# A scan with attention ahead of a mixture of experts: index casts paced, last routing cut finer, first slice halved, more identity products, fill split

## The chip, the cores and the metric

One core of a Trainium2 chip runs the program. The metric is the device time of one execution in microseconds (us); lower is better. The kernel before takes 640.82 us, the median of three runs (640.61 to 641.45).

## What is computed

Two stages follow each other. The first is a linear recurrence over 768 positions for 4 batches and 8 heads of 48 dimensions. Each position has a complex decay per dimension, normalised to a magnitude of at most 0.999; a 48x48 state per head is multiplied by it, the outer product of k and v is added, and the output is q times the state:

```
mag = sqrt(a_re**2 + a_im**2);  scale = minimum(mag, 0.999) / (mag + 1e-6)
for t: S = (a_re + i*a_im)*scale [t] * S + outer(k[t], v[t]);  y[t] = q[t] @ S.real
```

The outputs, seen as 3072 tokens of 384 values, go to the second stage. Each token picks the expert with the largest of 8 logits (x @ w_gate); an expert takes its tokens in order up to a capacity. A token's result is its gate weight times relu(x @ w1[e]) @ w2[e], with 1024 hidden values, and rows beyond the capacity give zero:

```
e = argmax(logits);  gate = softmax(logits)[e];  disp[e, counts[e]++] = x[i]
out[i] = gate[i] * (relu(disp @ w1[e]) @ w2[e])[row of i]
```

## The kernel before

The recurrence is done in chunks of 96 positions (8 chunks per batch). Inside a chunk it becomes an attention-like product, for which the running products of the decays from the chunk's middle are needed. They are made by a scan of 48 steps, for two chunks at a time: this is group g = 0 to 3, 128 partitions wide. A group is cut into six slices of eight steps. For each slice `norm` (lines 278 to 378) loads the decays (`a`), squares them (L305), sums real and imaginary squares (L310 on VectorE for the first slice of all, L272 by two products with the identity on TensorE for the others), takes logarithm and exponential on ScalarE (L329 to L348) and scales on VectorE (L344 to L364); L369 and L374 copy signs and real parts. `scan` (L404, L409) does the steps, one product and one sum each, every step after the one before. `post` multiplies q and k by the scanned products (L452 to L487) and writes them to a scratch in HBM (`scr<-qko`, issued by POOL). `pend` and `ends` hand the last products over.

The second part of a group is its eight units (`unit`, one batch of one chunk each): load q, k and v rows (`qkc<-scr`, issued by SP), transpose (L629), score (L645), mask (L649), the state (L660, L669, and the accumulating transfers `z<-sx`, L673, from POOL), outputs (L706, L711), gate logits (L924) and a transpose back into token rows (L911). The units of group g run beside the scan of group g + 1.

Tokens are routed in pieces, listed in `CUTS` as (group, units done): all eight units at once in groups 0 to 2, and 5, 1, 1 and 1 units in group 3. `routing` (L730) makes logits (L952), choice (L960 to L965), counts by products with ones (L970 to L975), slots (L983 to L986), gate weights (L996 to L1006) and then for each unit a one-column cast of the slot to an index (L1010, VectorE) and a scatter of its 96 rows into `disp` in HBM (L1024, an indirect transfer issued by POOL). The last three pieces (`LATE`) do not have to come back from HBM: the first expert's rows are read from `disp` once (`mload`, L1074, issued by SP after all scatters of the other pieces), and the rows of the late pieces are added by products (L1088) to the transposed ones (L1094). Before the scatters `disp` is filled with zeros by seven transfers (`fill`, L853, 772 KB each, from POOL).

Then the experts run one after the other with their weights split in two parts each (L1129, L1130): L1220 is the first product, L1266 and L1267 the relu, L1228 (L1241 for the last expert) the second product, and L1185 scatters finished rows to the output.

What sets the order is a planner. Every operation is entered with an engine, an estimated duration, a due time (`want`), what it comes after and the buffers that it uses. `solve` simulates the engines by these estimates and fixes the order of the instructions on every engine; at run time each engine works through its list and waits on semaphores. `apart` (L96) keeps an operation's planned start a given time behind that of another one; nothing of it remains at run time but the order. `BEGIN` holds the due times at which the groups' scans begin. `fill_gaps` (L158) puts products of the identity with itself (`keep`, L226) where TensorE's plan has a gap of more than 0.4 us, from planned time `begin` on. When operation 60 of the order has been written out, `tokens` and the routing's constants (lines 1508 to 1511) are written into every engine's list at that place. Up to there the memsets of `clear_ops` are written, one after every second operation, into POOL's list.

Of the kernel before, what the change touches and what calls it, by code (L numbers as in the profile page):

```python
# [7 lines left out]
F32 = mybir.dt.float32  # L8
# [17 lines left out]
SIZES = (8,) * 6  # L26
# [22 lines left out]
class Plan:  # L49
# [20 lines left out]
    def ready(self, o, by):  # L70
        r = o.start + o.dur
        if by.begun and o.kb is not None:
            return r
        if o.lat is not None:
            return r + o.lat
        return r + (self.OWN if o.eng == by.eng else self.LAT)[o.eng]
# [96 lines left out]
def dve(n):  # L173
    return .068 + n * .00104


def act(n):
    return .045 + n * .00086


class Att:
# [94 lines left out]
        return out  # L276

    def norm(self, g, j, s0):

        nc, plan = self.nc, self.plan  # L280
        n = SIZES[j]
# [22 lines left out]
                st[0] = sq[:, 0]  # L304
            nc.scalar.activation(sq, st['a'], AF.Square, accum_out=self.sums[g][:, 0, j:j + 1])  # L305
        o = plan.op(K + ("xa",), "ACT", act(2 * n * D) + .1, xa, w, after=[K + ("load",)], bufs=[a_, a4_])
        if g == 0 and j < 1:
            def xb():
                x = self.a4[g, j][:, 0:n, 3, :]
                nc.vector.tensor_tensor(out=x, in0=st['sq'][:, 0], in1=st['sq'][:, 1], op=ALU.add)  # L310
                st[0] = x
            o = plan.op(None, "DVE", dve(n * D), xb, w, after=[o], bufs=[a4_])
            parts = [(0, n, o, a4_)]
        elif by_dma:
            def acc():
                nc.gpsimd.dma_start(out=st['flat'][:, 0], in_=st['flat'][:, 1], accum_op=ALU.add)
            o = plan.op(K + ("acc",), "POOL", .6, acc, w - 2, after=[o], bufs=[a4_], kb=24 * n, extra=3.)
            parts = [(0, n, o, a4_)]
        else:
            parts = self.sums_of(plan, K, lambda: (st['sq'][:, 0], st['sq'][:, 1]), n, [o], w, st, [a4_])  # L320
# [60 lines left out]
    def scan(self, g, j, wants):  # L381

        nc, plan = self.nc, self.plan
        K = ("n", g, j)
        n = SIZES[j]
        a4_ = ("a4", g, j)
        for s in range(n - 1, -1, -1):
            if j == 0 and s == n - 1:
                continue
            st = {}  # L390
            prev = (g, j, s + 1) if s < n - 1 else (g, j - 1, 0)
            want = wants[STARTS[j] + s]

            def parts(o, f):
                for cs in ((slice(0, D),) if o.form == "full" else (slice(0, D // 2), slice(D // 2, D))):
                    f(cs)

            def mul(cs, s=s, st=st, prev=prev):
                a4 = self.a4[g, j]
                if 'xy' not in st:  # L400
                    st['xy'] = self.p_t.tile([128, 4, D], F32, tag="xy", name=f"xy_{g}_{j}_{s}", bufs=RINGS["xy"])
                w = self.a4[prev[0], prev[1]][:, prev[2], 0:2, cs]
                w = w.unsqueeze(1).broadcast_to([128, 2] + list(w.shape[1:]))
                nc.vector.tensor_tensor(out=st['xy'][:, :, cs].rearrange("p (u z) d -> p u z d", u=2),  # L404
                                        in0=a4[:, s, :, cs].rearrange("p (u z) d -> p u z d", u=2), in1=w, op=ALU.mult)

            def add(cs, s=s, st=st):
                xy = st['xy']
                nc.vector.tensor_tensor(out=self.a4[g, j][:, s, 0:2, cs], in0=xy[:, 0:4:2, cs], in1=xy[:, 1:4:2, cs], op=ALU.add)  # L409
            xy_ = ("xy", g, j, s)  # L410
            bufs = [a4_, xy_] + ([("a4", g, j - 1)] if s == n - 1 else [])
            before = [("s", g) + prev[1:]] if ("s", g) + prev[1:] in plan.names else []
            m = plan.op(None, "DVE", .27, None, want, after=before + [K + ("i",), K + ("r",)], bufs=bufs)
            a = plan.op(("s", g, j, s), "DVE", .169, None, want, after=[m], bufs=[a4_, xy_])
            m.fn, a.fn = lambda m=m, f=mul: parts(m, f), lambda a=a, f=add: parts(a, f)
            m.form = a.form = "?"
            m.full, m.part, a.full, a.part = .269, .338, .169, .24
            m.next, a.next = [a], []
            for x in before:
                plan.names[x].next.append(m)  # L420
# [309 lines left out]
    def routing(self, b, c, w, span):  # L730
        plan, rt = self.plan, self.route
        c0 = rt.begin(b, c)
        n = c + 1 - c0
        fs = rt.route(b, c0, c + 1)
        K = lambda s: ("r", b, c, s)
        W = n * E_
        gs, xs = ([("u", i % B, G2 * b + i // B, x) for i in range(c0, c + 1)] for x in ("G", "X"))
        s = span / 8
        t0, t1 = ("tr", "lg", b, c), ("tr", "pp", b, c)
        prev = [("r",) + PREV[b, c + 1] + ("run",)] if (b, c + 1) in PREV else []  # L740
        o = plan.op(None, "PE", .12 * n + .1, fs['logits'], w, after=gs, bufs=[t0])
        o = plan.op(None, "ACT", act(W) + .1, fs['lg'], w + s, after=[o], bufs=[t0])
        o = plan.op(None, "DVE", 4 * dve(W) + .1 + .5, fs['choose'], w + 2 * s, after=[o])
        o = plan.op(None, "PE", .2 * n + .3, fs['count'], w + 3 * s, after=[o] + prev, bufs=[t1])
        e = plan.op(None, "ACT", act(W) + .1, fs['exp'], w + 2 * s, after=[o])
        o = plan.op(K("slot"), "DVE", 4 * dve(W) + .4, fs['slot'], w + 4 * s, after=[o], bufs=[t1])
        plan.op(K("run"), "DVE", 2 * dve(W) + .2, fs['run'], w + 4.2 * s, after=[o])
        o = plan.op(K("place"), "DVE", 2 * dve(W) + 1.0, fs['place'], w + 4.5 * s, after=[o, e] + xs)
        for i in range(n):
            x = plan.op(None, "DVE", .12, fs['cast'][i], w + (5 + i) * s, after=[o])  # L750
            o_ = plan.op(K(("send", i)), "POOL", 1.0, fs['send'][i], w + (5 + i) * s, after=[x] + ([("mload",)] if (b, c + 1) in LATE else []), kb=148, extra=2.)
            if rt.scattered is not None:
                o_.apart = (rt.scattered, APART[b])
            rt.scattered = o_


RINGS = dict(qkc=3, v=3, qT=2, kT=2, a_sb=2, z=5, s_sb=4, sx=4, xt=2, tr=2, pa=2, s=1, ad=2, y=1,
# [1 line left out]
RINGS.update(raw=3, raw1=3, ends=1)  # L759
SLATE = 6  # L760
NACC = 4
BEGIN = (13, 67, 135, 203, 271)
FIRST = 8
BEHIND = 6
APART = (5, 5, 2.6, 1)


E_, F_ = 8, 1024
# [14 lines left out]
    return p, [min(p, w - t) for t in range(0, w, p)]  # L783


CUTS = [(0, 8), (1, 8), (2, 8), (3, 5), (3, 6), (3, 7), (3, 8)]
LATE = CUTS[-3:]
PREV = {b: (a[0], a[1] - 1) for a, b in zip(CUTS, CUTS[1:])}

# [247 lines left out]
class Moe:  # L1037
# [33 lines left out]
    def load(self):  # L1071

        nc = self.nc
        nc.sync.dma_start(out=self.xr, in_=self.disp[:T, :].rearrange("(t p) x -> p t x", p=TP))  # L1074
# [391 lines left out]
def kernel(ctx, tc, q, k, v, a_re, a_im, w_gate, w1, w2, av, xv, cen, vp, out):  # L1466
# [5 lines left out]
    with ExitStack() as c_main, ExitStack() as c_att:  # L1472
# [18 lines left out]
        box = {'route': route}  # L1491
        moe_plan(plan, box, early)
        for r in range(E_ * T // 512):
            plan.op(("fill", r), "POOL", .9, lambda r=r: box['fill'][r](), 9 + 3 * r, kb=772)
        order = plan.solve()
        plan.fill_gaps(att.keep)
        cut = max(i for i, o in enumerate(order) if o.idx < early) + 1
        with ExitStack() as c_moe:
            with ExitStack() as c_dve:
# [116 lines left out]
```

## Time and profile before

| | us |
|---|---|
| median of 3 runs | 640.82 |
| the profiled execution | 641.58 |
| its span, first to last instruction | 639.9 |

| engine | busy us | share of the span |
|---|---|---|
| TensorE (PE) | 561.8 | 88% |
| VectorE (DVE) | 458.9 | 72% |
| ScalarE (ACT) | 383.5 | 60% |
| GpSimd (POOL) | 212.9 | 33% |

The mean granted TensorE clock is 0.936 of 2.4 GHz. All times below are from the first instruction of the profiled execution on. A row of the timeline gives start, duration, engine, line, operation, output and inputs, the number of instructions merged into it, and in brackets how long its engine stood idle before it and what ended that. PEld is the load of TensorE's stationary operand, SPq and POOLq are the queues that issue transfers. "issue" is time in which an engine waited for nothing that the profile shows; "remote" marks a wait whose releaser is not seen on another engine.

### The profile page before, as it was taken

To read this page: it belongs to the slowest core of one execution; us is meant where nothing else is said; L and a number is where in the kernel's file an instruction comes from. 1 tells how busy PE (TensorE), PEld (TensorE's weight loads), DVE (VectorE), ACT (ScalarE), POOL (GpSimd) and SP (SyncE) were. 2 spreads that over 40 slices of the span, in tenths; PEclk is the share of its full clock that TensorE was granted. 3 is DMA by queue.
4 is the path that set the end of the run, shared out by engine and by line. 5 is a ranking of instruction groups with operands and counts; after the bars stand their busy time and mean duration, and the time that the engine had idled before them with its cause. 6 is when DMAs were issued, how large, how long until landed. Compare 5 with 4: busy or idle time off the path is not lost.

```text
span 639.9 us, 13273 instructions
## 1 busy us (share of the span) xinstructions
PE 561.8 (88%) x4662; PEld 489.7 (77%) x4662; DVE 458.9 (72%) x1340; ACT 383.5 (60%) x1034; POOL 212.9 (33%) x293
## 2 busy tenths in 40 slices
PE   2364569998999989999896889999999999999994
PEld 1122258786887868888785877999999999999993
DVE  3899979999999998999763244546665655655651
ACT  6465689989998899977652421344445344444540
POOL 9532314524459925464525031002020202112012
PEclk9666679999999999999999779999999999999997
DMA  6985588968899787885997231364545454455311
GB/s 214 297 245 147 147 203 231 241 189 207 196 230 251 213 228 168 213 223 135 215 242 209 55 91 29 109 184 125 163 129 158 138 169 155 155 165 159 101 37 37
DMA packets 75629, 108.81 MB, mean 170 GB/s; under 512 B 11716, under 2 KB 65853, under 8 KB 75553
## 3 DMA queue, kind: packets, MB, share of 16 engines
q1 hardware_dynamic: 58192, 57.37, 33.3%
q0 software_dynamic: 17360, 50.50, 29.1%
q8 instruction: 39, 0.64, 0.4%
q14 instruction: 38, 0.30, 0.2%
HBM read 71.51 MB, written 32.47 MB: 163 GB/s over the span
## 4 chain that ended last, share of the span: by engine, by line
PE 55%; DVE 20%; DMA 10%; ACT 9%; issue 4%; POOL 1%; POOLq 0%; DVEq 0%; ACTq 0%; SPq 0%
PE ph L1220 17%; PE my L1228 15%; DVE xy L404 4%; DMA scr<-qko 3%; DVE a L409 3%; PE pa L645 3%; PE tr L629 2%; DMA raw<-in_moe_w_dram 2%; PE n L272 2%; PE my L1241 2%; DMA qkc<-scr 2%; DVE qko L452 2%; PE s_all L660 2%; PE y L706 2%; DMA a<-in_av_dram 2%
## 5 line engine op out<-in xcount | busy, mean ns | idle before, releaser
L1266 ACT ACTIVATE hh<-ph 128x448 fp32r<-128x448 f32 (+7 forms) x64 | 32.7, 511 | 92.1 <-PE ph L1220 81.8
L1267 DVE SCALAR_TENSOR_TENSOR hl<-ph,hh 128x448 fp32r<-128x448 f32 (+7 forms) x64 | 37.2, 581 | 60.4 <-ACT hh L1266 59.6
L1185 POOL DMA_INDIRECT out_dram<-o,xr x26 | 25.7, 987 | 162.8 <-DVE o L1184 159.5
L1130 DVE TENSOR_TENSOR lo<-raw,hi 128x384 fp32r<-128x384 f32 (+2 forms) x128 | 65.7, 553 | 9.8 <-ACT hi L1129 9.7
L272 PE MATMUL n<-a,ident 128*128 128x384 f32 x92 | 44.8, 622 | 28.7 <-ACT a L305 28.7
L1220 PE MATMUL ph<-xh,hi 128*128 128x448 f32 (+7 forms) x192 | 69.5, 362 | 0.0
L1220 PE MATMUL ph<-xh,lo 128*128 128x448 f32 (+7 forms) x192 | 66.5, 347 | 0.0
L404 DVE TENSOR_TENSOR xy<-a 128x192 f32<-128x192 f32 (+1 forms) x199 | 61.5, 322 | 1.3 <-ACT a L374 1.1
L1129 ACT CAST hi<-raw 128x384 fp32r<-128x384 f32 (+2 forms) x128 | 59.1, 512 | 2.8 <-DMA raw<-in_moe_w_dram 2.8
L673 POOL DMA_DIRECT2D z<-sx x56 | 47.4, 1003 | 39.8 <-PE pa L645 12.4
L629 PE MATMUL tr<-ident,qkc 81*96 81x81 f32 x512 | 53.8, 241 | 5.6 <-DMA qkc<-scr 2.6
L1228 PE MATMUL my<-hh,lo 128*128 128x448 f32 (+6 forms) x168 | 58.7, 349 | 0.0
L1228 PE MATMUL my<-hh,hi 128*128 128x448 f32 (+6 forms) x168 | 58.6, 349 | 0.0
L1228 PE MATMUL my<-hl,hi 128*128 128x448 f32 (+6 forms) x168 | 58.6, 349 | 0.0
L649 DVE TENSOR_TENSOR a_sb<-pa,mask 96x384 f32<-96x384 f32 x64 | 35.1, 552 | 32.1 <-PE pa L645 21.1
L1024 POOL DMA_INDIRECT disp<-x,idx x32 | 42.1, 1315 | 46.1 <-DVE lm L961 22.4
L645 PE MATMUL pa<-qT,kT 128*96 128x96 f32 x512 | 56.9, 256 | 0.5 <-issue 0.4
L629 PEld LDWEIGHTS tr<-ident,qkc 81*96 81x96 f32 x512 | 43.3, 130 | 13.3 <-issue 4.0
L645 PEld LDWEIGHTS pa<-qT,kT 128*96 128x96 f32 x512 | 51.2, 170 | 2.5 <-issue 1.6
L272 PEld LDWEIGHTS n<-a,ident 128*128 128x128 f32 x92 | 20.0, 237 | 42.8 <-ACT a L305 24.6
L272 PE MATMUL p<-qko,ident 128*128 128x384 f32 x80 | 37.4, 598 | 15.3 <-ACT qko L441 15.2
L409 DVE TENSOR_TENSOR a<-xy 128x96 f32<-128x96 f32 (+1 forms) x218 | 49.8, 240 | 0.4
(224 smaller groups left out, 1459.0 us busy)
## 6 DMA issues: line engine op xcount, KB each, us to landing
raw<-in_moe_w_dram SPq DMA_DIRECT2D x64, 384.0 KB
qkc<-scr SPq DMA_DIRECT2D x32, 480.0 KB
scr<-qko POOLq DMA_DIRECT2D x44, 192.0 KB
scr<-qko POOLq DMA_DIRECT2D x20, 384.0 KB
a<-in_av_dram POOLq DMA_DIRECT2D x18, 384.0 KB
qkin<-in_xv_dram POOLq DMA_DIRECT2D x18, 384.0 KB
disp<-fill POOLq DMA_DIRECT2D x7, 772.0 KB
v<-in_vp_dram SPq DMA_DIRECT2D x32, 144.0 KB
```

The source lines that it names most:

```text
L272: nc.tensor.matmul(out=pt[:, :m], lhsT=self.ident, rhs=t[:, h:h + m], start=i == 0, stop=i == 1)
L404: nc.vector.tensor_tensor(out=st['xy'][:, :, cs].rearrange("p (u z) d -> p u z d", u=2), in0=a4[:, s, :, cs].rearrange("p (u z) d -> p u z ...
L409: nc.vector.tensor_tensor(out=self.a4[g, j][:, s, 0:2, cs], in0=xy[:, 0:4:2, cs], in1=xy[:, 1:4:2, cs], op=ALU.add)
L629: nc.tensor.transpose(out=pt[:, h * C:h * C + NE], in_=qk[:NE, 4 * hh + h, z_ * C:z_ * C + C], identity=self.ident[:NE, :NE])
L645: nc.tensor.matmul(out=pa[:, h * C:h * C + C], lhsT=kT[:, 4 * hh + h], rhs=qT[:, 4 * hh + h], start=True, stop=True)
L673: nc.gpsimd.dma_start(out=zn[a.start:a.stop or C], in_=st['sx'][o], accum_op=ALU.add)
L1024: ins = nc.gpsimd.indirect_dma_start(out=self.disp, out_offset=bass.IndirectOffsetOnAxis(ap=idx[:, c:c + 1], axis=0), in_=self.row(b, c0 + ...
L1129: return (lambda: nc.scalar.copy(out=hi[i][:, s], in_=raw[i][:, s]), lambda: nc.vector.tensor_tensor(out=lo[i][:, s], in0=raw[i][:, s], in ...
L1130: lambda: nc.vector.tensor_tensor(out=lo[i][:, s], in0=raw[i][:, s], in1=hi[i][:, s].bitcast(F32), op=ALU.subtract))
L1220: nc.tensor.matmul(out=ph[:, :W], lhsT=a[:, k, fs], rhs=r[:, k, :W], start=i == 0, stop=i == len(parts) - 1)
L1228: nc.tensor.matmul(out=py[m][:, :W], lhsT=a[:, f % self.PF, ms], rhs=r[:, :W], start=f == 0 and i == 0, stop=f == NF - 1 and i == 2)
L1267: nc.vector.scalar_tensor_tensor(out=hl[:, :W], in0=ph[:, :W], scalar=0.0, in1=hh[:, :W].bitcast(F32), op0=ALU.max, op1=ALU.subtract)
```

## The change

- The distance `apart` is taken between the casts of the indices on VectorE, no longer between the scatters on POOL, and its values for groups 2 and 3 go from 2.6 and 1 to 2 and 1.4 us.
- The first routing of group 3 takes four units, and the fifth gets a piece of its own (`CUTS`).
- The first slice of group 0 has a function of its own, `norm_first`: it loads and normalises the eight steps in two halves of four, upper half first; every operation of `norm` for that slice is done twice on half the columns, and a scan step waits for its own half only.
- The groups' due times begin 3 us earlier (`BEGIN`).
- Identity products fill planned gaps from planned time 58 on, not 82.
- The seven fills have due times of their own (`FILL`).

```diff
     def norm(self, g, j, s0):
+        if g == 0 and j == 0:
+            self.norm_first(s0)
+        else:
+            self.norm_slice(g, j, s0)
+
+    def norm_first(self, s0):
...
+        n = SIZES[0]
+        w = s0 - 10
...
+        for p, h in enumerate(range(n - HALF, -1, -HALF)):
+            i = slice(h, h + HALF)
+            m = HALF * D
+            v = w + 4 * p
+
+            def load(i=i, p=p):
+                if p == 0:
+                    tiles_()
+                nc.sync.dma_start(out=st['a'][:, :, i], in_=self.av[0][:, :, STARTS[0] + i.start:STARTS[0] + i.stop, :])
+
+            def xa(i=i, p=p):
+                sq = st['a4'][:, i, 0:2, :].rearrange("p i z d -> p z i d")
+                nc.scalar.activation(sq, st['a'][:, :, i], AF.Square, accum_out=sums[:, 0, NS + p:NS + p + 1])
...
+            o = plan.op(K + ("load", p), "SP", .6, load, v - 14, bufs=[a_], kb=48 * HALF, extra=2.)
+            o = plan.op(K + ("xa", p), "ACT", act(2 * m) + .1, xa, v, after=[o], bufs=[a_, a4_])
+            x_ = plan.op(None, "DVE", dve(m), xb, v, after=[o], bufs=[a4_])
+            o = plan.op(None, "ACT", act(m), xc, v, after=[x_], bufs=[a4_, ln_, c0_, t5_])
+            e = plan.op(None, "ACT", act(m), xe, v, after=[o], bufs=[ln_, c0_])
+            o = plan.op(None, "ACT", act(m) + .1, xq, v, after=[e], bufs=[ln_, c0_])
+            o = plan.op(None, "DVE", dve(m), mm, v + 4, after=[o], bufs=[a4_, ln_])
+            t = plan.op(None, "ACT", act(m), tt, v + 4, after=[e], bufs=[c0_, t5_])
+            o = plan.op(None, "DVE", dve(m), c1, v + 5, after=[o, t], bufs=[ln_, c0_])
+            o = plan.op(None, "DVE", dve(m), sc, v + 6, after=[o, t], bufs=[c0_, t5_])
+            oi = plan.op(None, "DVE", dve(m), mi, v + 7, after=[o], bufs=[a_, t5_, a4_])
+            orr = plan.op(None, "DVE", dve(m), mr, v + 7, after=[o], bufs=[a_, t5_, a4_])
+            plan.op(K + ("i", p), "ACT", act(m) + .08 * (p == 0), ci, v + 7.5, after=[oi], bufs=[a4_])
+            plan.op(K + ("r", p), "ACT", act(m), cr, v + 7.5, after=[orr], bufs=[a4_])
...
+        def ready(s):
+            p = ((n - 1 - s) // HALF,) if g == 0 and j == 0 else ()
+            return [K + ("i",) + p, K + ("r",) + p]
...
-            m = plan.op(None, "DVE", .27, None, want, after=before + [K + ("i",), K + ("r",)], bufs=bufs)
+            m = plan.op(None, "DVE", .27, None, want, after=before + ready(s), bufs=bufs)
...
             x = plan.op(None, "DVE", .12, fs['cast'][i], w + (5 + i) * s, after=[o])
-            o_ = plan.op(K(("send", i)), "POOL", 1.0, fs['send'][i], w + (5 + i) * s, after=[x] + ([("mload",)] if (b, c + 1) in LATE else []), kb=148, extra=2.)
+            plan.op(K(("send", i)), "POOL", 1.0, fs['send'][i], w + (5 + i) * s, after=[x] + ([("mload",)] if (b, c + 1) in LATE else []), kb=148, extra=2.)
             if rt.scattered is not None:
-                o_.apart = (rt.scattered, APART[b])
-            rt.scattered = o_
+                x.apart = (rt.scattered, APART[b])
+            rt.scattered = x
...
-BEGIN = (13, 67, 135, 203, 271)
+FILL = (9, 13, 17, 21, 43, 47, 62)
+HALF = 4
+BEGIN = (10, 64, 132, 200, 268)
...
-APART = (5, 5, 2.6, 1)
+APART = (5, 5, 2, 1.4)
...
-CUTS = [(0, 8), (1, 8), (2, 8), (3, 5), (3, 6), (3, 7), (3, 8)]
+CUTS = [(0, 8), (1, 8), (2, 8), (3, 4), (3, 5), (3, 6), (3, 7), (3, 8)]
...
-            plan.op(("fill", r), "POOL", .9, lambda r=r: box['fill'][r](), 9 + 3 * r, kb=772)
+            plan.op(("fill", r), "POOL", .9, lambda r=r: box['fill'][r](), FILL[r], kb=772)
         order = plan.solve()
-        plan.fill_gaps(att.keep)
+        plan.fill_gaps(att.keep, begin=58.)
```

## Rows read from the trace of the kernel before

**Rows 1.** Windows: stretch and its length, then busy us (instructions) by engine, clock, DMA.

```profile
23.00:72.00 49.00, 23.15 (x37) 10.75 (x38) 48.64 (x174) 30.08 (x63) 14.81 (x28) 0.67 0.70 205
72.00:92.00 20.00, 13.10 (x49) 8.24 (x49) 16.38 (x54) 14.16 (x35) 6.29 (x9) 0.63 0.89 221
92.00:345.00 253.00, 241.95 (x2837) 205.35 (x2836) 232.20 (x702) 211.44 (x644) 129.67 (x154) 0.99 0.84 209
345.00:352.00 7.00, 1.34 (x10) 0.93 (x10) 0.00 (x0) 0.42 (x1) 5.33 (x6) 0.84 0.69 221
352.00:360.00 8.00, 6.39 (x60) 5.82 (x60) 1.11 (x2) 2.78 (x9) 0.00 (x0) 0.50 0.36 89
360.00:374.00 14.00, 13.88 (x192) 12.32 (x189) 7.42 (x43) 6.66 (x21) 2.77 (x3) 1.00 0.11 33
...
399.00:632.00 233.00, 231.69 (x1316) 225.20 (x1314) 133.95 (x285) 99.65 (x221) 28.52 (x30) 1.00 0.45 135
```

**Rows 2.** Timeline from 342 to 353 us: first and last of eight scatters, then what follows.

```profile
342.19 1.04 POOL L1024 DMA_INDIRECT disp<-x,idx  x1 [0.30 <-DVE a_sb L649]
...
350.93 0.92 POOL L1024 DMA_INDIRECT disp<-x,idx  x1 [0.30 <-issue]
351.58 0.48 ACT L900 COPY xt<-y 128x384 f32<-128x384 f32 x1 [8.34 <-remote]
...
352.12 0.55 PE L924 MATMUL y<-xt,wg 128*32 128x96 f32 x8 [5.37 <-issue]
```

**Rows 3.** Timeline from 375 to 390 us: last of five scatters, read-back, its first use.

```profile
375.38 0.92 POOL L1024 DMA_INDIRECT disp<-x,idx  x1 [0.30 <-ACT qT L633]
...
377.99 0.32 SPq L1074 DMA_DIRECT2D xr<-disp  x1
...
389.50 1.12 PE L1094 MATMUL mt<-ident,xr 112*128 112x112 f32 x8
```

**Rows 4.** Timeline of L924, once per unit, after the row of 352.12.

```profile
361.58 0.37 PE L924 MATMUL y<-xt,wg 128*32 128x96 f32 x8
...
367.10 0.37 PE L924 MATMUL y<-xt,wg 128*32 128x96 f32 x8
...
379.18 0.55 PE L924 MATMUL y<-xt,wg 128*32 128x96 f32 x8
...
385.75 0.37 PE L924 MATMUL y<-xt,wg 128*32 128x96 f32 x8
```

**Rows 5.** Timeline: first and last of four scatters among the experts; the window around them.

```profile
584.87 0.95 POOL L1185 DMA_INDIRECT out_dram<-o,xr  x1 [21.70 <-DVE o L1184]
...
589.90 0.94 POOL L1185 DMA_INDIRECT out_dram<-o,xr  x1 [0.30 <-issue]
...
584.00:591.00 7.00, 7.00 (x45) 6.92 (x43) 4.21 (x9) 1.80 (x4) 3.79 (x4) 1.00 0.77 231
```

**Rows 6.** Timeline of the start, then groups by line: count, busy us and mean ns.

```profile
4.72 0.84 ACT L305 ACTIVATE a<-a 128x768 f32<-128x768 f32 x1 [2.61 <-DMA a<-in_av_dram]
...
13.04 0.43 DVE L404 TENSOR_TENSOR xy<-a 128x96 f32<-128x96 f32 x2 [1.12 <-ACT a L374]
...
21.10 0.23 POOL L837 IOTA tok<- 96x32 int32 x1
...
22.38 0.25 DVE L242 TENSOR_TENSOR mask<-ptok,tokrow 96x96 f32<-96x96 f32 x1 [2.33 <-ACT tokcol L241]
...
L853 POOL DMA_DIRECT2D disp<-fill x7 | 5.7, 863 | 0.0
L487 DVE TENSOR_TENSOR qko<-a,v 128x768 f32<-128x768 f32 x6 | 5.7, 957 | 0.0
L344 DVE TENSOR_TENSOR lnn<-n,lnn 128x384 f32<-128x384 f32 x7 | 3.9, 553 | 0.0
```

**Rows 7.** Chain of waits: the sums' products at the handover, and later.

```profile
74.45 2.93 PE n L272 x4
...
127.64 1.35 PE n L272 x4
```

More of the change, by code (lines that the diff above doesn't have):

```diff
@@ L278, in norm, with tiles_, xb, xc @@
     def norm(self, g, j, s0):
+        if g == 0 and j == 0:
[3 more added lines that the diff above has]
+    def norm_first(self, s0):
+        nc, plan = self.nc, self.plan
+        n = SIZES[0]
+        w = s0 - 10
+        K = ("n", 0, 0)
+        sums = self.sums[0]
+        st = {}
+        def tiles_():
+            st['a4'] = self.tile_a4(0, 0)
+            st['a'] = self.p_in.tile([128, 2, n, D], F32, tag="a", name="a_0_0", bufs=RINGS["a"])
+            for x in ("ln", "c0", "t5"):
+                st[x] = self.p_t.tile([128, n, D], F32, tag=x, name=f"{x}n_0_0", bufs=RINGS[x])
+        a_, a4_, ln_, c0_, t5_ = ("a", K), ("a4", 0, 0), ("ln", K), ("c0", K), ("t5", K)
+        for p, h in enumerate(range(n - HALF, -1, -HALF)):
[9 more added lines that the diff above has]
+                nc.scalar.activation(sq, st['a'][:, :, i], AF.Square, accum_out=sums[:, 0, NS + p:NS + p + 1])
+            def xb(i=i):
+                nc.vector.tensor_tensor(out=st['a4'][:, i, 3, :], in0=st['a4'][:, i, 0, :], in1=st['a4'][:, i, 1, :], op=ALU.add)
+            def xc(i=i):
+                nc.scalar.activation(st['ln'][:, i], st['a4'][:, i, 3, :], AF.Ln, bias=self.b_tiny)
+            def xe(i=i):
+                nc.scalar.activation(st['c0'][:, i], st['ln'][:, i], AF.Exp, bias=self.b_lncap, scale=-0.5)
+            def xq(i=i):
+                nc.scalar.activation(st['ln'][:, i], st['c0'][:, i], AF.Square, scale=1.0 / CAP,
+                                     accum_out=sums[:, 1, self.col[0]:self.col[0] + 1])
+                self.col[0] += 1
+            def mm(i=i):
+                nc.vector.tensor_tensor(out=st['ln'][:, i], in0=st['a4'][:, i, 3, :], in1=st['ln'][:, i], op=ALU.mult)
+            def tt(i=i):
+                nc.scalar.activation(st['t5'][:, i], st['c0'][:, i], AF.Identity, bias=self.b_half, scale=0.5e-6 / CAP)
+            def c1(i=i):
+                nc.vector.scalar_tensor_tensor(out=st['c0'][:, i], in0=st['ln'][:, i], scalar=-3.0, in1=st['c0'][:, i], op0=ALU.add, op1=ALU.mult)
+            def sc(i=i):
+                nc.vector.scalar_tensor_tensor(out=st['t5'][:, i], in0=st['c0'][:, i], scalar=-2.0, in1=st['t5'][:, i], op0=ALU.max, op1=ALU.mult)
+            def mi(i=i):
+                nc.vector.scalar_tensor_tensor(out=st['a4'][:, i, 2, :], in0=st['a'][:, 1, i], scalar=self.sign[:, 0:1], in1=st['t5'][:, i],
+                                               op0=ALU.mult, op1=ALU.mult)
+            def mr(i=i):
+                nc.vector.tensor_tensor(out=st['a4'][:, i, 0, :], in0=st['a'][:, 0, i], in1=st['t5'][:, i], op=ALU.mult)
+            def ci(i=i, p=p):
+                k = i.stop - (p == 0)
+                nc.scalar.mul(out=st['a4'][:, i.start:k, 1, :], in_=st['a4'][:, i.start:k, 2, :], mul=-1.0)
+                if p == 0:
+                    nc.scalar.copy(out=st['a4'][:, k, 1, :], in_=st['a4'][:, k, 2, :])
+            def cr(i=i):
+                nc.scalar.copy(out=st['a4'][:, i, 3, :], in_=st['a4'][:, i, 0, :])
+            o = plan.op(K + ("load", p), "SP", .6, load, v - 14, bufs=[a_], kb=48 * HALF, extra=2.)
[12 more added lines that the diff above has]
+            plan.op(K + ("r", p), "ACT", act(m), cr, v + 7.5, after=[orr], bufs=[a4_])
@@ L280, in norm, with norm_slice @@
+    def norm_slice(self, g, j, s0):
         nc, plan = self.nc, self.plan
@@ L306, in norm @@
         o = plan.op(K + ("xa",), "ACT", act(2 * n * D) + .1, xa, w, after=[K + ("load",)], bufs=[a_, a4_])
[L307 to L314, printed above, removed]
+        if by_dma:
             def acc():
```

## The prediction

> **What bounds the kernel now.** I read the windows by stage first. In the experts TensorE is busy 231.69 of 233 us and the change touches nothing there, so that stage is a constant. Before it there are four stages [rows 1]. From 23 to 72 us VectorE is the bound: 48.64 of 49 us busy, TensorE less than half. From 72 to 92 us nobody is full: that is the handover from the first scan to the first units, at a granted clock of 0.63. From 92 to 345 us TensorE is busy 241.95 of 253 us and VectorE 232.20, so a start that comes earlier is passed on here, neither lost nor enlarged. From 345 to 399 us comes the surprise: in the seven microseconds to 352 VectorE does nothing, ScalarE 0.42 and TensorE 1.34 us, and the eight after it run at clock 0.50, while 360 to 374 shows TensorE busy 13.88 of 14 at 1.00.
>
> The timeline tells what goes on beside that hole. POOL issues eight scatters in one train, from 342.19 to 351.85, (350.93 - 342.19) / 7 = 1.25 us apart, since all eight indices were cast together; ScalarE's next copy starts at 351.58 after 8.34 us of idleness with no releaser on another engine, TensorE's next work at 352.12 after 5.37 us of "issue" [rows 2]. What stops the engines is not named by any view; I go by the coincidence, which comes twice: a train of five scatters ends at 376.30, and the unit it falls into is long again [rows 3, 4]. L924 runs once per unit and serves as a clock: 352.12, 361.58, 367.10, 379.18, 385.75, so the units last 9.46, 5.52, 12.08 and 6.57 us [rows 2, 4].
>
> **The change, part by part.** All sums are on the profiled execution, 641.58 us; its span is 639.9.
>
> *Casts paced, routing in pieces of four and one.* No cast is added; each moves down VectorE's list, to planned distances of 2 us (group 2) and 1.4 us (group 3), and POOL's scatter waits for its own. Does a train with such distances still stop the others? The trace has no such train in this stage. The nearest row is among the experts: four scatters start between 584.87 and 589.90, 1.68 us apart on the mean, and TensorE is busy 7.00 of 7.00 us around them [rows 5]. So at 2 us I expect no hole, and at 1.4 us a smaller one.
>
> What the holes cost: take 5.52 us as a unit without disturbance; it even contains a five-unit routing. The first hole is 7.00 - 1.34 = 5.66 us of TensorE, and the slow unit behind it 9.46 - 5.52 = 3.94; together 9.6. The second costs 12.08 - 5.52 = 6.56 and 6.57 - 5.52 = 1.05; together 7.6. All of it is 17.2 us, the upper end; the lower is 0. I take the first whole (8 scatters spread over 14 us) and half of the second, 3.8, because four scatters may still come in a row at 1.4 us: 13.4 us gained.
>
> The piece more is one more round of choice, counts, slots and weights on VectorE (idle half of 360 to 374, 7.42 of 14 [rows 1]) and two pairs of small products. 6.57 - 5.52 = 1.05 us is the most that a unit with a one-unit routing shows [rows 4]; between 0 and that I take 0.4 us lost.
>
> What the pacing could make late: the scatter waits for its cast, and behind it on POOL wait the state's transfers and the scratch writes; on SP `mload` waits for the last scatter of the early pieces. In groups 0 and 1 the planned 5 us were the scatters' own before; VectorE is nearly full there, so a cast that slips holds POOL, which is busy 129.67 of 253 us [rows 1]: 0, at most about 2 us. In group 3 the read-back is issued at 377.99 and first used at 389.50, 11.5 us later [rows 3]. With TensorE 13.4 us earlier that cover would be gone, but the fifth unit's piece now needs one scatter instead of five, and the four start one unit, 5.5 us, earlier; I count 0 and keep up to 3 us for the range.
>
> *First slice in two halves.* From the first square at 4.72 to the first scan step at 13.04 there are 8.3 us of operations one behind the other [rows 6]. On VectorE 768 columns take 0.957 and 384 take 0.553 us, so 192 take some 0.553 - 0.202 = 0.35, 0.63 of the whole. The chain shrinks to 5.3 us, and half a load may land 0.5 us sooner: the scan starts 3.5 us earlier. The second halves cost VectorE six times 2 x 0.35 - 0.553 = 0.15, 0.9 us, in time that it idles. But the constants stand in every list at operation 60, and the 14 operations more push that place forward. VectorE reached it at 20.05 and waited 2.33 us [rows 6]. Half of 14 operations at some 0.35 us is 2.5; with the 3.5 of the start it arrives at about 14. POOL finishes the last constant at 21.10 + 0.23; with three fills of 0.86 us fewer ahead of it, at 18.7 [rows 6]. So the wait grows to nearly 5 us. It ends 3.5 to 4 us earlier than before, with two scan steps and three scaling operations (2.4 us) still to do. Net 1.5 us gained; between -1 (POOL not earlier) and 3.5 (no wait).
>
> *Fills.* Seven as before, 0.86 us each on POOL; three move from 15-27 us to 43-62, where VectorE is the bound and POOL is busy 14.81 of 49 us [rows 1]. Beyond the constants' wait they are worth nothing: 0, with up to 0.5 either way inside the range above.
>
> *Identity products from 58 on.* They go into TensorE's idle time ahead of 72 us and through the handover. There the sums' products take 2.93 us on the chain and 1.35 at the higher of the two clocks (1.2 and 2.4 GHz) [rows 7]; two such sets (74.45 and 85.62) lie on the chain, 3.2 us. Upper end: half of TensorE's 13.10 us, 6.5. Lower end: -1, if the products themselves run at the low clock and hold up a sum behind them. ScalarE (14.16 of 20) and the read-back of the first units, with DMA at 0.89, are next [rows 1], so I take 2.0.
>
> In 72 to 92 us TensorE also does transposes. The Trainium skill, page "TensorE: Matmul & The Clock Gate", section "Part 4: PE-mode transpose", says that transposes do not count as activity for the clock. From 352 to 360 us TensorE was busy 6.39 of 8 us, transposes among it, and stayed at 0.50 [rows 1], which fits but does not separate it. By that rule the second set falls back to the low clock and the term is half, 1.0.
>
> *Sum.* 13.4 - 0.4 + 1.5 + 2.0 = 16.5; 641.58 - 16.5 = 625.1. The profiled execution is 0.76 above the median, so I say 624.3 for the median.
>
> **The rivals.** *The second train still stops the engines* (four at 1.4 us are close to the 1.25 of before; for it: the distance hardly grew; against: rows 5): 3.8 less, 628.1.
>
> *The casts bunch.* The pace exists only in the plan; if VectorE waits for TensorE with several casts behind the wait, they come together and POOL sends a train as before. For it: from 360 to 374 VectorE idles half its time [rows 1]. Against: each wait lets through only what stands between two masks. Then only start and clock remain: 641.58 - 3.5 + 0.4 - 0.76 = 637.7.
>
> *The transposes keep the handover slow* (above): 625.3.
>
> *Slower: every scatter stops the others while POOL writes it, whatever the distance.* In place of two holes there would be 13 of 0.92 us, 12.0 us, and TensorE interrupted every 2 us would stay at the low clock, 3.94 us for each unit. It beats the 17.2 us of now, and the 3.5 of start and clock, from (17.2 + 3.5 - 12.0) / 3.94 = 2.2 units on; over four units it is 12.0 + 15.8 = 27.8: 641.58 + 27.8 - 17.2 - 3.5 + 0.4 - 0.76 = 648.3. Against: the four scatters of rows 5 leave TensorE full.
>
> *The change does not do what it says*: the plan puts the casts apart and VectorE's order shows it, so I give that nothing beyond the bunching.
>
> **How the numbers follow.** My forecast 56%, the transposes' rival 10%, the second train 17%, bunching 10%, slower 7%. Low end: 17.2 + 3.5 + 3.2 = 23.9 gained, 616.9. High end: the bunching's 637.7, cut to 637; what is left out is the slower case and the worse half of bunching with a poor start. The likeliest case's own range is 619 to 631. About 0.2%, 1.3 us, is what a measurement here tells from no change. Faster by more: 56 + 10 + 17 and most of bunching, 0.89. Within 0.2%: bunching with the start lost, 0.04. Slower: 0.07.
>
> **What would show it.** Right: scatters of group 2 start 2 us apart, ScalarE shows no "remote" waits of several us, L924 comes every 5 to 6 us, the clock stays at 1.00 from 340 on; the first scan step is at 9 to 10 us, the wait at the mask near 5 us; sums near 1.4 us at the handover. Wrong: scatters 1.2 us apart, or holes despite the distance; the read-back's first use waiting for its landing; a stage 92 to 345 that grows by what its start gained.

## The result and the profile after

The changed kernel takes 623.96 us (median of 4 runs, 623.83 to 624.21) against 640.98 us (640.61 to 641.45) on the same chip: ratio 0.9735, 95% interval 0.9718 to 0.9751. Its profiled execution takes 624.08 us, with a span of 622.3 and a mean granted clock of 0.962. The forecast was 624.3.

In the profile after, the functions of the units and the routing stand 90 lines further down (L924 is L1014, L900 is L990, the scatter is L1114), masks are at L737 and scan steps at L492. Here are the windows that answer to [rows 1]; the experts now begin 17.9 us earlier.

```profile
72.00:92.00 20.00, 18.50 (x151) 15.36 (x150) 19.25 (x56) 17.18 (x45) 5.58 (x8) 0.96 0.85 226
345.00:352.00 7.00, 6.77 (x92) 6.08 (x88) 3.65 (x24) 3.29 (x12) 2.74 (x3) 1.00 0.42 119
352.00:360.00 8.00, 5.29 (x78) 4.76 (x78) 3.40 (x22) 2.82 (x10) 3.68 (x4) 1.00 0.20 59
360.00:374.00 14.00, 13.10 (x165) 11.51 (x164) 7.98 (x50) 4.54 (x15) 3.66 (x4) 1.00 0.34 97
```

Two things jump out. From 72 to 92 us TensorE went from 13.10 to 18.50 of 20 us and from clock 0.63 to 0.96; 7.0 of the 18.50 are identity products, of which the kernel before has none there. This group of instructions is from the window 72 to 92 us (count, busy us, mean ns):

```profile
L226 PE MATMUL s_all<-ident 128*128 128x128 f32 x47 | 7.0, 303 | 0.0
```

And the great hole is gone: TensorE has 6.77 of 7 us in the window to 352, at 1.00. A smaller one is left from 352 to 360, with 5.29 of 8. The timeline shows what lies in it (answer to [rows 2]): three scatters that do come together (the last of group 2's eight and the first two of group 3), and ScalarE and VectorE idle until 0.8 us after the last has ended.

```profile
353.08 0.92 POOL L1114 DMA_INDIRECT disp<-x,idx  x1 [2.05 <-DVE sl L1073]
354.49 0.93 POOL L1114 DMA_INDIRECT disp<-x,idx  x1 [0.49 <-DVE se L1088]
355.75 0.92 POOL L1114 DMA_INDIRECT disp<-x,idx  x1 [0.33 <-issue]
357.51 0.48 ACT L990 COPY xt<-y 128x384 f32<-128x384 f32 x1 [4.79 <-remote]
357.67 0.55 DVE L737 TENSOR_TENSOR a_sb<-pa,mask 96x384 f32<-96x384 f32 x1 [2.71 <-remote]
358.05 0.37 PE L1014 MATMUL y<-xt,wg 128*32 128x96 f32 x8 [2.33 <-ACT xt L990]
```

The scatters of group 2 are not evenly 2 us apart: their eight starts lie between 336.94 and 353.08, 1.27 to 3.85 us from one to the next. The first three stand 1.56 and 1.27 us apart, a first triplet.

At the start (answer to [rows 6]) the first square is at 3.87 and the first scan step at 10.25; the constants cost VectorE two waits of under 1 us.

```profile
3.87 0.52 ACT L311 ACTIVATE a<-a 128x384 f32<-128x384 f32 x1 [1.76 <-DMA a<-in_av_dram]
10.25 0.36 DVE L492 TENSOR_TENSOR xy<-a 128x192 f32<-128x192 f32 x1 [0.23 <-ACT a L353]
17.29 0.25 DVE L242 TENSOR_TENSOR mask<-ptok,tokrow 96x96 f32<-96x96 f32 x1 [0.79 <-ACT tokcol L241]
18.44 0.26 DVE L920 CAST dec<-ii 96x8 f32<-96x8 int32 x1 [0.90 <-POOL ii L917]
```

Three marks divide the gain: the third unit's first product (114.41 before, 109.08 after), the first product of the unit into which the train falls (L924 at 338.65, L1014 at 333.89), and the experts' first product (399.14 and 381.22). Here they are in the timeline, three before and three after:

```profile
114.41 0.37 PE L924 MATMUL y<-xt,wg 128*32 128x96 f32 x8
338.65 0.37 PE L924 MATMUL y<-xt,wg 128*32 128x96 f32 x8
399.14 0.45 PE L1220 MATMUL ph<-xh,hi 128*128 128x448 f32 x1
109.08 0.37 PE L1014 MATMUL y<-xt,wg 128*32 128x96 f32 x8
333.89 0.37 PE L1014 MATMUL y<-xt,wg 128*32 128x96 f32 x8
381.22 0.45 PE L1310 MATMUL ph<-xh,hi 128*128 128x448 f32 x1
```

So 5.3 us come from before 114 us, of which 4.8 are still there at 338.65; the scatter stage between the last two marks shrinks from 60.49 to 47.33 us, 13.2; the experts take 240.8 and 241.1 us. 4.76 + 13.16 - 0.32 = 17.60, the difference of the spans.

### The profile page after: what moved, and what is told of

It is laid out like the page before. It is cut to its first block, busy times and chain, and to the rows that moved or that the text cites. A ratio compares the mean times of both kernels' runs of the same rounds, so it can differ in the third digit from the quotient of the medians.

```text
span 622.3 us, 13489 instructions
## 1 busy us (share of the span) xinstructions
PE 558.7 (90%) x4740; PEld 491.0 (79%) x4740; DVE 462.7 (74%) x1366; ACT 383.6 (62%) x1045; POOL 209.5 (34%) x293
## 4 chain that ended last, share of the span: by engine, by line
PE 54%; DVE 19%; ACT 14%; DMA 5%; POOL 3%; issue 2%; another core or an unknown queue 1%; POOLq 0%; ACTq 0%; SPq 0%; DVEq 0%
PE ph L1310 17%; PE my L1318 15%; DVE xy L492 4%; DVE a L497 3%; ACT z L768 3%; PE pa L733 2%; DMA scr<-qko 2%; PE my L1331 2%; PE tr L717 2%; DVE qko L540 2%; ACT ends L615 2%; PE s_all L748 2%; PE y L794 1%; PE yt L1264 1%; DVE qko L575 1%
## 5 line engine op out<-in xcount | busy, mean ns | idle before, releaser
L492 DVE TENSOR_TENSOR xy<-a 128x192 f32<-128x192 f32 (+1 forms) x202 | 61.3, 318 | 0.8 <-ACT a L353 0.2
L272 PE MATMUL n<-a,ident 128*128 128x384 f32 x92 | 41.6, 585 | 16.9 <-POOL qT L246 8.9
L733 PE MATMUL pa<-qT,kT 128*96 128x96 f32 x512 | 55.0, 251 | 0.7 <-ACT kT L721 0.7
L717 PE MATMUL tr<-ident,qkc 81*96 81x81 f32 x512 | 52.5, 237 | 3.0 <-ACT x L1007 1.3
L1114 POOL DMA_INDIRECT disp<-x,idx x32 | 40.3, 1260 | 39.8 <-ACT lt L1017 9.5
L733 PEld LDWEIGHTS pa<-qT,kT 128*96 128x96 f32 x512 | 49.5, 166 | 2.9 <-ACT kT L721 1.1
L717 PEld LDWEIGHTS tr<-ident,qkc 81*96 81x96 f32 x512 | 41.6, 127 | 9.7 <-ACT x L1007 2.4
L737 DVE TENSOR_TENSOR a_sb<-pa,mask 96x384 f32<-96x384 f32 x64 | 35.1, 549 | 15.3 <-PE pa L733 10.9
L1310 PE MATMUL ph<-xl,hi 128*128 128x448 f32 (+7 forms) x192 | 45.8, 346 | 0.0
```

What stands on the lines that cost most here:

```text
L272: nc.tensor.matmul(out=pt[:, :m], lhsT=self.ident, rhs=t[:, h:h + m], start=i == 0, stop=i == 1)
L717: nc.tensor.transpose(out=pt[:, h * C:h * C + NE], in_=qk[:NE, 4 * hh + h, z_ * C:z_ * C + C], identity=self.ident[:NE, :NE])
L733: nc.tensor.matmul(out=pa[:, h * C:h * C + C], lhsT=kT[:, 4 * hh + h], rhs=qT[:, 4 * hh + h], start=True, stop=True)
L1114: ins = nc.gpsimd.indirect_dma_start(out=self.disp, out_offset=bass.IndirectOffsetOnAxis(ap=idx[:, c:c + 1], axis=0), in_=self.row(b, c0 + ...
L1310: nc.tensor.matmul(out=ph[:, :W], lhsT=a[:, k, fs], rhs=r[:, k, :W], start=i == 0, stop=i == len(parts) - 1)
```

## The experiments

Theory A is the prediction's: a train of scatters 1.25 us apart stops the other engines by itself. Its main rival, formed after the runs on chip 10 and called theory C from r2_before on, is that the stop is a condition of the chip or of the execution which a train meets or does not. (Rivals B and C in the expectations of e1 to e4 are others: that the finer pieces, or the start and the handover, bring the gain.) The runs went to chips 10, 5, 1 and 3 in that order, each chip once, and each has its own times of the kernel before; only ratios on one chip compare. The times expected for e1 to e4 were meant for the chip of the result, so on chip 10 their mechanisms can be tested, but not their microseconds.

**e1, trains again.** Casts together, distances on the scatters, as before the change; all else of the change stays.

```diff
-            plan.op(K(("send", i)), "POOL", 1.0, ...
+            o_ = plan.op(K(("send", i)), "POOL", 1.0, ...
             if rt.scattered is not None:
-                x.apart = (rt.scattered, APART[b])
-            rt.scattered = x
+                o_.apart = (rt.scattered, APART[b])
+            rt.scattered = o_
...
-APART = (5, 5, 2, 1.4)
+APART = (5, 5, 2.6, 1)
```

> The changed kernel with the distance back on the scatters (and its values 2.6 and 1), so that all indices of a piece are cast together; all else stays. Theory A (a train of scatters stops the other engines, and the distance between the casts is what takes the trains apart): the holes come back behind the eight scatters of group 2 and, smaller, behind the four of group 3; 633 to 637 us, with ScalarE waits marked remote of 5 us and more. Rival B (the finer pieces of the last routing bring the gain): within 2 us of the changed kernel, 622 to 626. Rival C (start and clock at the handover bring it): the same, 622 to 626.

Measured on chip 10: 620.28 us, ratio 0.9914 (0.988 to 0.9947), where the kernel before takes 626.3. The scatters come 1.22 us apart again (first two rows: from the middle of the train in the timeline), yet the windows around them show TensorE full, and no "remote" wait occurs:

```profile
342.64 0.92 POOL L1114 DMA_INDIRECT disp<-x,idx  x1 [0.30 <-issue]
343.86 0.92 POOL L1114 DMA_INDIRECT disp<-x,idx  x1 [0.31 <-issue]
...
345.00:352.00 7.00, 6.94 (x99) 6.34 (x97) 3.63 (x23) 4.03 (x12) 3.75 (x5) 1.00 0.74 219
352.00:360.00 8.00, 7.97 (x123) 7.28 (x123) 5.22 (x28) 3.96 (x13) 4.51 (x5) 1.00 0.33 95
```

What it would have cost on the chip of the result, this run can't say.

**e2, five units in the first piece.** All else of the change stays.

```diff
-CUTS = [(0, 8), (1, 8), (2, 8), (3, 4), (3, 5), (3, 6), (3, 7), (3, 8)]
+CUTS = [(0, 8), (1, 8), (2, 8), (3, 5), (3, 6), (3, 7), (3, 8)]
```

> The changed kernel with the first routing of group 3 over five units again, casts still paced. Theory A: five paced scatters are little worse than four and one; 624 to 627 us. Rival B (the pieces matter, since the read-back of the first expert's rows waits for fewer scatters): 629 us or more, with the first product on the read-back rows waiting for their landing. Rival C: 623 to 625.

Measured on chip 10: 621.87 us, ratio 0.9941 (0.992 to 0.9961). The scatter stage takes 44.5 us; with pieces of four and one it takes 43.0 in e3 and 42.5 in e4, which pace the casts as e2 does. So the piece more is no cost.

**e3, no identity products in the first scan.**

```diff
-    plan.fill_gaps(att.keep, begin=58.)
+    plan.fill_gaps(att.keep, begin=82.)
```

> The changed kernel with identity products from planned time 82 on as before. Theory A: the handover falls back to the low clock, the sums' products there take 2.9 us again, and it costs the 2 us that the two traces differ by at the handover; 625 to 627 us. Rival C (the clock at the handover is a main source): 629 us or more. Rival B: 624.

Measured on chip 10: 625.06 us, ratio 0.9969 (0.9932 to 1.0006). First the window of the handover and the third unit's first product of e3, then those of e2, which has the products:

```profile
72.00:92.00 20.00, 14.44 (x75) 9.91 (x76) 17.23 (x49) 14.61 (x39) 5.57 (x8) 0.70 0.79 211
111.52 0.37 PE L1014 MATMUL y<-xt,wg 128*32 128x96 f32 x8
```

```profile
72.00:92.00 20.00, 17.24 (x148) 13.88 (x150) 19.35 (x56) 17.42 (x45) 5.57 (x8) 1.00 0.85 227
108.96 0.37 PE L1014 MATMUL y<-xt,wg 128*32 128x96 f32 x8
```

Without them the clock of the stretch is 0.70 instead of 1.00 and the third unit's first product comes 2.6 us later. That much is the products' own (predicted 2.0).

**e4, the first slice whole.** `norm_first` is no longer called, the first slice's sum is on VectorE as before the change, and the due times of the groups are the old ones.

```diff
-        if g == 0 and j == 0:
-            self.norm_first(s0)
-        else:
-            self.norm_slice(g, j, s0)
+        self.norm_slice(g, j, s0)
...
-BEGIN = (10, 64, 132, 200, 268)
+BEGIN = (13, 67, 135, 203, 271)
```

> The changed kernel with the first slice in one piece and the groups' due times 3 us later, as before. Theory A: the first scan ends some 2.8 us later, as in the two traces, and this is handed on to the end; 625.5 to 628 us. Rival C (the start is a main source): 630 us or more. Rival B: 624.

Measured on chip 10: 619.53 us, ratio 0.9898 (0.9855 to 0.9941). The first scan starts 2.8 us later again (13.02 against 10.25 in the kernel after), and the third unit's first product comes at 109.35 us all the same, where e2, with the halves, has 108.96: 0.4 us is lost without them.

**Chip 5: before, after, trains, pacing alone.** Since no hole showed up on chip 10, the next runs are both kernels, unchanged, with profiles of their own (r2_before, r2_after), e1 once more (r2_trains), and the kernel before with the pacing as its only edit (r2_pace_alone):

```diff
-            o_ = plan.op(K(("send", i)), "POOL", 1.0, ...
+            plan.op(K(("send", i)), "POOL", 1.0, ...
-                o_.apart = (rt.scattered, APART[b])
-            rt.scattered = o_
+                x.apart = (rt.scattered, APART[b])
+            rt.scattered = x
...
-APART = (5, 5, 2.6, 1)
+APART = (5, 5, 2, 1.4)
```

> The kernel before, unchanged, with a profile of its own on the chip that the other three share. Theory C (the two long stops at the trains of scatters are a condition of the chip or of the execution, which the train of scatters meets or does not): where the time is near 641 the first product of the unit after the train comes over 3 us late and PE is busy under 6 of 7 us in 345:352; where it is near 626 the late stage has no hole over 1 us. Theory A (eight scatters 1.24 us apart stop the other engines whatever the chip): both holes are there, 13 us of idle PE, wherever it runs.

> The kernel after, unchanged. Theory A: 17 us below the kernel before on this chip, as on the first one (ratio 0.973). Theory C: the same 17 us only if the kernel before shows its two holes on this chip; without them only the start and the handover to the second scan are left of the change, 2.8 and 2.2 us, less up to 2 us for the paced casts and the unit more, so 3 to 5 us (ratio 0.992 to 0.995).

> The kernel after with the distances put back on the scatters (all eight casts at once, distances 5, 5, 2.6 and 1), again, now beside the kernel after on one chip. Theory A: 10 to 13 us above the kernel after. Theory C: where the kernel before has no holes, 0 to 3 us below the kernel after, since its triplets of scatters leave holes of 1 to 2 us and evenly spaced ones none; where the kernel before has them, 8 to 13 us above.

> The kernel before with only the pacing of the index casts added (distance on the casts, 5, 5, 2 and 1.4); pieces of the last group, first slice, identity products and fill as before. Theory A: 10 to 13 us below the kernel before. Theory C: the same where the kernel before has its holes, otherwise within 2 us of the kernel before, on either side.

Measured on chip 5, where the kernel before takes 625.13 us (19 runs): before again 1.0004 (0.9982 to 1.0026), after 618.89 us or 0.9886 (0.9868 to 0.9903), trains 618.97 us or 0.9894 (0.9877 to 0.991), pacing alone 624.9 us or 0.9997 (0.9972 to 1.0022). So on this chip the pacing brings nothing in either kernel, and the whole change brings 6.2 us, somewhat more than theory C's 3 to 5. The profile of r2_before, timeline and windows, stands against [rows 1, 2]:

```profile
341.20 1.04 POOL L1024 DMA_INDIRECT disp<-x,idx  x1 [0.30 <-DVE a_sb L649]
...
343.54 0.48 ACT L900 COPY xt<-y 128x384 f32<-128x384 f32 x1 [1.29 <-PE y L711]
344.76 0.37 PE L924 MATMUL y<-xt,wg 128*32 128x96 f32 x8
...
349.94 0.92 POOL L1024 DMA_INDIRECT disp<-x,idx  x1 [0.30 <-ACT qT L621]
...
345.00:352.00 7.00, 7.00 (x107) 6.46 (x99) 2.08 (x4) 4.16 (x12) 4.59 (x5) 1.00 0.93 292
352.00:360.00 8.00, 7.97 (x107) 7.10 (x106) 5.01 (x32) 4.08 (x14) 1.10 (x2) 1.00 0.01 3
```

It is the same program, and the same train to a hundredth of a us: (349.94 - 341.20) / 7 = 1.25. But ScalarE makes its copy 2.3 us after the first scatter starts, not 9.4 us, and TensorE is full through the train. Theory A falls here. Of the 15.9 us between the two profiled executions of the kernel before (641.58 and 625.67) 15.7 lie in the scatter stage, 60.49 against 44.83 us.

**Chip 1: does the pacing pay where the holes are?** The kernel after, e4 again, and e4 with the trains of e1 (the two diffs together).

> The kernel after, unchanged, for the two others to stand beside. Theory C (the stops of the other engines during the scatters come with the chip or the execution): 6 to 7 us below the kernel before where that takes about 626 us, 17 us below where it takes about 641. Theory A (trains stop the others always) is down to this: it would need 13 us of idle PE in every profile of the kernel before.

> The kernel after with the first slice whole again and the old due times of the groups (13, 67, 135, 203, 271). If the halves are worth what the prediction gave them, 1.5 us above the kernel after. If the handover to the second scan is bounded by PE's products alone (first product of the third unit 109.35 us here, 109.08 to 109.24 in the kernel after), within 0.6 us of it, on either side.

> The kernel after with the first slice whole and the distances back on the scatters (casts all at once, 5, 5, 2.6, 1): only the identity products in the first scan, the finer last unit and the new fill are left of the change. Theory C: where the kernel before shows no stops, within 1 us of the whole-slice kernel and of the kernel after; where it shows them, 8 to 13 us above both, with waits on something outside the core in its profile. Theory D (the pacing is worth its cost for a reason of its own, such as fewer stalls of the casts' engine): 2 us or more above the whole-slice kernel on any chip.

Measured on chip 1, where the kernel before takes 641.99 us (14 runs): after 624.16 us or 0.9738 (0.971 to 0.9765), whole slice 622.81 us or 0.9721 (0.9691 to 0.975), whole slice with trains 637.31 us or 0.993 (0.9901 to 0.9959). So the trains cost 14.5 us here, the same edit that cost nothing in the kernel after on chip 5. The whole slice itself isn't told from the kernel after. The profile of the trains, r3_whole_trains, has the hole back; timeline and windows:

```profile
340.07 1.03 POOL L1118 DMA_INDIRECT disp<-x,idx  x1 [0.30 <-DVE a_sb L741]
...
348.78 0.92 POOL L1118 DMA_INDIRECT disp<-x,idx  x1 [0.30 <-issue]
350.92 0.48 ACT L994 COPY xt<-y 128x384 f32<-128x384 f32 x1 [9.94 <-remote]
351.45 0.55 PE L1018 MATMUL y<-xt,wg 128*32 128x96 f32 x8 [6.75 <-issue]
351.76 0.55 DVE L741 TENSOR_TENSOR a_sb<-pa,mask 96x384 f32<-96x384 f32 x1 [11.02 <-remote]
...
345.00:352.00 7.00, 0.55 (x8) 0.20 (x8) 0.24 (x1) 0.82 (x3) 3.68 (x4) 0.57 0.45 134
352.00:360.00 8.00, 7.86 (x65) 7.37 (x66) 1.79 (x7) 2.92 (x11) 0.00 (x0) 0.53 0.32 79
```

A stop is paid twice: the idle 6.75 us, and eight us behind it in which TensorE is full but at the lower of its two clocks, 0.53. The kernel after has on this chip what it had in the result, the "remote" waits of 4.8 and 2.7 us at its triplet of scatters; the whole slice has one of 2.7 (and one of 0.3). In none of the eight profiles from chips 10 and 5 does a "remote" wait occur.

**r4, the last casts further apart.** The triplet comes from VectorE's order: the last cast of group 2 stands just ahead of a masked product and the first two of group 3 behind it, before the next one. With 2.2 us a masked product stands between those two as well. On top of e4:

```diff
-APART = (5, 5, 2, 1.4)
+APART = (5, 5, 2, 2.2)
```

> The kernel after with the first slice whole, the old due times, and the distances of the last two groups at 2 and 2.2 in place of 2 and 1.4, so that the casts of the last group lie one masked product apart in VectorE's order, where three of them stood within one before. Theory C, where the kernel before takes about 641 us: the stop of about 2.5 us that was left in 352:360 shrinks, 1 to 3 us below the whole-slice kernel (ratio 0.967 to 0.971). Where the kernel before takes about 626 us: nothing is left to gain, ratio 0.987 to 0.991, and a cast that is held back further may cost up to 1 us at the last scatter. Rival: a scatter that stands alone stops the others as long as one in a train, and the stops only move; then the ratio stays at 0.972 to 0.975 on the first kind of chip.

Measured on chip 3, where the kernel before takes 638.76 us: 622.68 us, ratio 0.9715 (0.967 to 0.976). The stop at 352 to 360 is gone, with the three scatters 1.67 and 2.41 us apart; the one at the first three scatters, still 1.3 us apart, stays (r4_even, scatters and windows):

```profile
351.67 0.92 POOL L1118 DMA_INDIRECT disp<-x,idx  x1 [1.98 <-DVE sl L1077]
353.34 0.93 POOL L1118 DMA_INDIRECT disp<-x,idx  x1 [0.75 <-DVE ok L1099]
355.75 0.92 POOL L1118 DMA_INDIRECT disp<-x,idx  x1 [1.47 <-ACT x L1011]
...
338.00:345.00 7.00, 6.03 (x89) 5.33 (x85) 2.16 (x9) 3.11 (x10) 1.83 (x2) 1.00 0.69 186
345.00:352.00 7.00, 6.46 (x82) 5.92 (x83) 4.27 (x26) 3.61 (x13) 3.07 (x4) 1.00 0.31 88
352.00:360.00 8.00, 8.00 (x128) 7.15 (x123) 4.76 (x34) 4.17 (x14) 3.54 (x5) 1.00 0.25 72
```

In time this is not told from the whole slice on chip 1 (0.9721), and the two profiles are from different chips: they fit the mechanism, but a gain isn't shown. Of the versions tried none beats the kernel after by more than the intervals.

## Why the prediction was right, and where it was not

The forecast of 624.3 us came true at 623.96, and the split into 13.0 us from the scatters and 3.5 from start and handover came out as 13.2 and 4.8. The terms behind it are less good than the sum. And part of it is luck: the result was measured where the stops occur, as in the trace that the forecast was read from. On chip 5 the same change brings 6.2 us, not 17.

**Holes, predicted 13.4.** That pacing removes the stops is shown, on chip 1 by whole slice against whole slice with trains. Their size had to be estimated from a unit taken as undisturbed, 5.52 us. The kernel before on chip 5 gives the units without stops, one by one; here is the scatter stage of four profiles, cut at the first products of its units (before, those of [rows 2, 4]) and ended by the experts' first:

| us | first unit | second | third | fourth | fifth | rest | stage |
|---|---|---|---|---|---|---|---|
| before, chip of the result | 13.47 | 9.46 | 5.52 | 12.08 | 6.57 | 13.39 | 60.49 |
| before, chip 5 | 7.09 | 4.97 | 5.52 | 7.86 | 4.43 | 14.96 | 44.83 |
| after, chip of the result | 8.09 | 4.94 | 11.13 | 4.21 | 8.04 | 10.92 | 47.33 |
| after, chip 5 | 6.81 | 4.91 | 8.23 | 4.20 | 6.92 | 11.30 | 42.37 |

The stops cost 6.38 + 4.49 = 10.9 us at the first train (predicted 9.6) and 4.22 + 2.14 = 6.4 at the second (predicted 7.6), less 1.6 given back behind them: 15.7 together, where the upper end was 17.2. After the change 47.33 - 42.37 = 5.0 us of stops are left: 1.3 in the unit of the first triplet, 2.9 in that of the second, 1.1 in the fifth. By this reckoning the pacing is worth 15.7 - 5.0 = 10.7, not 13.4. It rests on four single profiles from two chips; the direct pair on chip 1, the whole slice with and without trains, gives 14.5 us between the medians and 10.2 between the profiled executions (635.37 and 625.2). So the term is right in kind, and 13.4 is not shown to be too much. That it would be worth nothing on another chip was in none of the rivals: I took a coincidence seen twice in one execution for a property of the train.

**The piece more, predicted -0.4.** This sign was wrong. Without stops the stage takes 44.2 to 44.8 us with a first piece of five units (r2_before, r2_pace_alone, e2), and 42.0 to 43.0 with four and one (r2_after, r2_trains, e1, e3, e4); between runs that both pace the casts on one chip the gain is 1.5 to 2.0 us (e2 against e3 and e4, r2_pace_alone against r2_after). I had priced the extra instructions and counted 0 for the read-back. But without stops its first use is what TensorE waits for. In r2_before the read-back is issued at 367.88, after the last scatter of the five has landed, in r2_after at 363.50, after that of the fifth unit's own piece. The first products that use it, in the one and in the other:

```profile
372.86 1.12 PE L1094 MATMUL mt<-ident,xr 112*128 112x112 f32 x8 [1.44 <-DMA xr<-disp]
368.18 1.12 PE L1184 MATMUL mt<-ident,xr 112*128 112x112 f32 x8 [0.24 <-DMA xr<-disp]
```

From the start of the stage that is 35.2 and 32.4 us. In r2_pace_alone TensorE doesn't stand there, since the plan has put identity products in the gap (28 of them, 3.6 us, from 369.24 on).

The two profiles of chip 5 differ by 44.83 - 42.37 = 2.5 us in this stage, and 10.7 + 2.5 makes the 13.2. By that reckoning two errors of nearly 3 us cancelled; by the direct pair on chip 1 they may be smaller.

**Halves, predicted 1.5, identity products, predicted 2.0.** The wait at the constants should have grown to 5 us; it is 0.79 + 0.90. POOL's last constant was there about when I said (VectorE goes on at 18.44; I had 18.7), but VectorE came to the mask at 16.5, not at 14. That is 3.6 us earlier than the 20.05 of before; I had added 2.5 for the place that moves forward to 3.5 for the start. The first scan's last state is copied at 68.56 us instead of 71.35, 2.8 earlier. Yet this gain isn't kept: with the products and whole slices the third unit starts at 109.25 us on chip 1, with halves at 108.99, 0.3 us. The two terms are not independent. Against the 114.41 and 113.12 us of the kernel before, halves without products give 111.52, products without halves 109.35 on chip 10, both 109.08. What holds the third unit back once the products are in was not tested. TensorE's 18.50 of 20 us in the handover don't show it to be full of work, since 7.0 of them are identity products; VectorE, busy 19.25 of the 20 us where it was 16.38 before, is nearer to a bound.

**Transposes at the handover.** The rival that the second set of sums falls back to the low clock is out; in the kernel after these products take 1.56 us where [rows 7] shows 2.93:

```profile
84.14 1.56 PE L272 MATMUL n<-a,ident 128*128 128x384 f32 x4 [0.16 <-ACT a L396]
```

The page's rule on transposes (the Trainium skill, "TensorE: Matmul & The Clock Gate", "Part 4: PE-mode transpose") isn't refuted by that, since ordinary products lie between the transposes here.

**The other rivals and the signs.** "Casts bunch" was partly right: three scatters did come 1.41 and 1.26 us apart, and this triplet stopped the engines for 2.3 us of TensorE, not for the full hole. "The second train still stops" names the same remnant. "Every scatter stops the others" is out: the scatters that stand alone in r4 at 351.67 to 355.75 leave TensorE at 8.00 of 8. Of the signs, the clock of 1.00 from 340 us on and the sums at the handover came true. That there would be no "remote" wait of several us and a unit every 5 to 6 us did not: there is one of 4.79 us, and the units take 4.21 to 11.13.

**What stays open.** Why trains stop the other engines on chip 1 (and, by its times and its first triplet, on chip 3) and not on 5 and 10. It is not the single execution: the kernel before took 638.1 to 646.4 us in all 25 runs on chips 1 and 3 and 622.9 to 632.1 in all 50 on chips 5 and 10. But each of these chips was measured in one stretch only, and the number of the result's own chip is not on record, so what differs may be the chip or something that lasted as long as its runs did. The view says "remote", that is, no engine's record ends the wait. POOL itself keeps its distances throughout, and the traffic doesn't differ as the train begins: 912 packets and 0.86 MB in three us in both profiles of the kernel before (343 to 346 us on the chip of the result, 342 to 345 on chip 5). In the hole itself it is less, not more: 701 packets from 345 to 352 us, where r2_before has 1583 from 344 to 351. Whether the engines waited for instructions wasn't tested; of those packets one belongs to the instruction queues in the hole and two in r2_before, but no view says when an instruction was asked for. ScalarE stands 4.79 us in the kernel after and 9.94 in r3_whole_trains. The Trainium skill, "SBUF — State Buffer", "SBUF: two separate sides", names only one contention among the engines' ports, VectorE and GpSimd on their shared pair, and says that TensorE and ScalarE never wait on anyone there; a ScalarE that stands as long as VectorE is not that. No run took the writing of the scatters apart from their data.

## What to carry to other kernels

A hole with no named releaser is worth a second profile on another chip before it is explained: the same program, with the same train, lost 15.7 us on one chip and nothing on another. Pacing is still right, as it cost nothing on chip 5, where the stops don't occur, and saved 14.5 us on chip 1, where they do. Two edits that both feed the same handover are not to be added up, and a piece of work cut finer should be priced by what waits for its last part, not only by its extra instructions.

## What the runs showed that was not expected

The time of a program on one core differs between chips by far more than between runs on one: the kernel before takes 641.0, 642.0 and 638.8 us in three measurements and 625.1 and 626.3 in two, and on chip 5 its third unit and the start of its scatter stage lie within 1.3 us of those on the chip of the result.

A long stop is paid again in clock: after the 6.75 us of r3_whole_trains TensorE has the next eight us at 0.53, eight products taking 0.55 us where 0.37 is usual, as in [rows 2, 4]. After the 2.33 us stop of the kernel after the clock stays at 1.00. The length of the stop alone does not decide it, though: in r3_whole_slice TensorE stops for 1.60 us, and the window around it is at 0.87.

```profile
352.00:360.00 8.00, 5.65 (x71) 5.12 (x72) 3.17 (x21) 2.80 (x10) 3.68 (x4) 0.87 0.21 63
```
